# Attention and long-convolution kernel: block parameters and exponents in one load each, query scores copied to SBUF before their maximum is subtracted

## The chip, the cores and the metric

The kernel runs on one core of a Trainium2 chip. The core has five engines that run side by side, each with its own instruction queue in program order: TensorE (PE, matrix products into PSUM; PEld is its weight load), VectorE (DVE), ScalarE (ACT), GpSimd (POOL) and SyncE (SP), which here issues every DMA. They wait for one another through semaphores. The metric is the device time of one execution in microseconds (us).

## What is computed

Two independent layers over 2048 positions and 576 channels; their outputs stand side by side in the result.

```python
def _A_ref(u, log_A_real, A_imag, C_real, C_imag, log_dt, D_skip):
    dt = jnp.exp(log_dt)
    A = -jnp.exp(log_A_real) + 1j * A_imag
    C = (C_real + 1j * C_imag) * dt[:, None]
    P = jnp.exp((A * dt[:, None])[:, :, None] * pos[None, None, :])
    K = 2.0 * jnp.einsum("dn,dnl->dl", C, P).real          # 128 states n
    y = irfft(rfft(u_t, 4096) * rfft(K, 4096))[:, :, :2048]  # long convolution
    return y + u * D_skip

def _B_ref(x, wqkv, w_phi, wo):                 # 32 heads of 18
    q, k, v = split_heads(x @ wqkv)
    pq, pk = q @ w_phi, k @ w_phi               # per head
    phi_q = concat([softmax(pq), softmax(-pq)])
    phi_k = concat([softmax(pk), softmax(-pk)])
    kv, z = phi_k^T v, sum(phi_k)
    return (phi_q kv / (phi_q z + 1e-6)) @ wo
```

## The kernel before

**Attention layer.** The positions are cut into 16 tiles of 128. First `fold` multiplies `w_phi` into the key weights, and `whole` loads the value weights; each weight is split into a high part `wh` and a low part `wl` so that the fast float format keeps its precision. A key tile (`key_tile`) loads x (`zo`), splits it into the nine blocks `x9`, makes its scores and values in three matrix products of 14 passes each (378, 378 and 396 columns), takes both softmaxes (`softmax`) and adds its part to the state `kvt` with 32 small matmuls (`e,v` in the profile). After the sixteenth, the query weights are folded. A query tile (`query_tile`) makes its scores in two products of 288 columns, goes through `softmax(..., total=True)`, turns the result (L678), multiplies it with the state (`kvb,fT`), divides, turns it again (L706, L707) and multiplies with `wo`.

In `softmax`, DVE reads a half of the scores from PSUM three times: L568 takes the negated maximum, L569 the minimum, L570 (helper line L450) adds the negated maximum and writes the tile `e` in SBUF. L574 makes the mirrored half from it, L576 is the exponential on ACT.

**Convolution layer.** 144 matrices of 128 states are worked in 36 groups of four channels (`group`). A group's phases are made by integer additions on POOL (L888), turned into sines and cosines on ACT (L912 to L916), and weighted by magnitudes: three matmuls of the exponents `mg` with a selection matrix `sel` (L929), an exponential on ACT (L930) and four multiplications on DVE (L936 to L941). 64 small matmul passes (`E,cs`) make the group's part of the filter. Six blocks of six groups share parameters: `params` loads four rows of numbers per block (`dt`, `th`, `cre`, `cim`) with four DMAs and works on them with some forty small instructions; `exponents` loads `mg` twice, into the upper and the lower 64 partitions, from the array `gd` in device memory. The filter goes through a first transform step (`k_first`), u through `u_first`, then come 16 `product` blocks and 16 `last` blocks.

**What sets the order.** Nothing runs in the order in which it is written. A planner (`Plan.run`) holds all operations with their dependencies and costs and places them one after the other; each unit has a due time in the table `WANT`, each step of a unit an offset in `LEAD`, and `STAY`, `TURNOVER`, `NEAR`, `LEAN_POOL` and `LEAN_ACT` weigh the choices. An operation that names two engines (`copy("any", ...)`: ACT or DVE; `FLEX` and other pairs: DVE or POOL) is put where the planner sees it end first. Where the planner sees PE wait for the input of a new PSUM tile, it fills the wait with matmuls on zeros (L215, `ps<-ident,zero` in the profile), which compute nothing that is used. Each engine then runs its list in that fixed order.

Of the kernel before, what the change touches and what calls it, by code (L numbers as in the profile page):

```python
# [19 lines left out]
H, DH = 32, 18  # L20
# [28 lines left out]
def layouts(i):  # L49
# [4 lines left out]
    for g, n in enumerate(GRP):  # L54
# [3 lines left out]

    twice = lambda x: np.concatenate([x, x[512:]])
    lar, cre, cim = i["A_log_A_real"], i["A_C_real"], i["A_C_imag"]  # L60
    return dict(
        u=c(i["A_u"][0].reshape(64, 16, 2, D).transpose(2, 0, 1, 3).reshape(128, 16 * D)), mag=np.stack([by_row(x) for x in (lar, cre, cim)]), ldt2=by_row(i["A_log_dt"][:, None]), aim=by_group(i["A_A_imag"]), cre=by_group(i["A_C_real"]),
        cim=by_group(i["A_C_imag"]), ldt=by_group(i["A_log_dt"][:, None])[0], dsk=c(i["A_D_skip"]),
# [4 lines left out]
def constants():  # L68
# [56 lines left out]
    none = np.zeros_like(at)  # L125
    sel = np.concatenate([np.concatenate([at, none, dn], 1), np.concatenate([none, up, none], 1)])
# [25 lines left out]
class Mark(Buf):  # L152


    def __init__(self):
        self.tag, self.writers, self.readers = None, [], []


class Plan:
# [26 lines left out]
    def op(self, eng, cost, fn, r=(), w=(), with_=(), early=0.0, table=None, busy=1.0, lock=False, mode=(128, 128), add=None):  # L186
# [12 lines left out]
        bufs = list({id(b): b for b in (*r, *w, *with_) if not isinstance(b, Mark)}.values())  # L199
# [176 lines left out]
def c_dma(nbytes, run=4096):  # L376
    return nbytes / run * (0.35 + 0.0029 * run)
# [5 lines left out]
STAY, TURNOVER, NEAR, LEAN_POOL, LEAN_ACT = 201.0337, 32.8045, 106.7441, -80.6454, 62.4245  # L383
LEAD = dict(g1=-171.8003, g2=572.2435, g3=151.3761, g4=545.6015, k1=48.5812, k2=-375.6500, k3=-757.7275, k4=-640.2771, l1=-1201.2185, p1=-789.5548, p2=-44.7091, p3=-18.2983, p4=-535.3487, q1=82.0847, q2=-177.3983, q3=-254.3079, q4=-403.9251, q5=-398.9575, q6=-829.6788, u1=458.1288, xd=-783.9802)
# [4 lines left out]
    ident=[-108.8011],  # L389
    fold=[-9953.8356, -10398.4174, -453.1777, 165.8967],  # L390
    start=[1616.5931],
    key=[-6472.8031, -3126.8062, -1314.3574, -3125.3684, -656.72, -499.3546, -3140.1215, -1712.5806, -2108.3757,
          -1097.3828, -995.3063, -3475.5769, -5054.2771, -1149.402, -2645.614, -12059.5893],
    kv=[-10.1299],
    query=[5165.3029, 1080.554, 692.3202, 1735.0859, -197.7761, 3588.2092, 2132.912, 435.8626, 2776.5646, 4448.3212,
          4159.3881, 4303.4831, 5219.083, 4714.8471, 4446.1239, 3107.4294],
    u=[-1640.9461, -3267.9218, -4820.103, -2553.3502, -977.4058, -3531.8924, -390.5478, -577.8274, -2654.6962,
          -4160.3913, -2177.6267, -4468.1255, -741.7491, -4170.1538, -4622.046, -4241.0767],
    mags=[-9388.2816],
    sel=[-7210.3842, -4975.1123, -11383.6242],  # L400
    dsk=[2087.7151],
    par=[-11102.6929, -5509.5329, -1199.9769, -424.7275, 1524.2103, 2698.0598],
    group=[-7457.0019, -5406.6149, -4731.1573, -4251.2752, -3514.0599, -2749.8781, -3073.1041, -3256.4294, -3042.7242,
          -2141.1152, -1003.1983, -2662.6797, -315.8551, -156.0662, 211.9443, 4253.1033, 2854.2949, 574.2642],
    kfirst=[-4429.7629, -1297.4347, -385.4741, 1666.6694],
    product=[-90.1674, 1697.6391, -210.3218, 1304.2139, 977.2179, -172.77, 437.5617, -517.2988, 1754.78, 1904.223,
          3993.8576, 2617.1633, 3713.9029, 3193.0326, 3608.0088, 3162.4523],
    last=[2342.2332, 1752.2374, 2676.4796, 653.6455, 734.6483, 754.2121, 126.96, 2202.2106, 3127.1116, 3903.7028,
          3067.4349, 3943.3771, 2944.3536, 3914.8745, 4473.7986, 2888.4515],
)  # L410


def body(tc, nc, i, out, ctx):
    pl = Plan()
# [704 lines left out]
```

## Time and profile before

| | |
|---|---|
| three runs | 588.89, 586.17, 588.4 us, median 588.4 |
| profiled execution, own time | 588.28 us |
| its span, first to last instruction | 586.5 us |
| PE, DVE, ACT, POOL busy | 556.6, 513.1, 389.5, 251.8 us |
| zero matmuls of L215 | 193, busy 27.74 us of PE's 556.6 |
| mean granted TensorE clock | 0.991 |

"Busy" counts from the start of an instruction to its end, with overlaps counted once. Matmuls overlap, so the start-to-start distance says what one more costs. The page's slices are fortieths of the span (14.7 us); a digit 9 means 90% busy or more. The chain is the row of pieces of work, each released by the one before, that ended last. In the views of groups the columns are line, engine, operation, tiles, shapes and count; then busy time and mean length of one; then the idle time before them.

### The profile page before, as it was taken

Reading aid. Unit: us, or ns where it says so; the run is one execution under the profiler, and the core shown is the slowest. Engines: PE = TensorE matmul, PEld = TensorE weight load, DVE = VectorE, ACT = ScalarE, POOL = GpSimd, SP = SyncE. Lnnn points to the kernel's source line nnn. Section 1 sums busy time; section 2 is a strip of 40 time slices with the busy share of each in tenths; the row PEclk is TensorE's granted clock in tenths of the full one; section 3 lists DMA queues with packets and bytes.
Section 4 is the critical chain, followed back from the end, with each engine's and each line's share of the span. In section 5 each row is a group of like instructions: output and inputs, shape, how many; then the busy total and the mean of one; then the engine's idle time right before and its main releaser. Section 6 shows DMA issues by size and latency. Waiting matters only on the chain.

```text
span 586.5 us, 18741 instructions
## 1 busy us (share of the span) xinstructions
PE 556.6 (95%) x7657; PEld 457.9 (78%) x7657; DVE 513.1 (87%) x1109; ACT 389.5 (66%) x666; POOL 251.8 (43%) x393
## 2 busy tenths in 40 slices
PE   5998999999999899899999999999999999999996
PEld 3998989898879688778888766676788876767884
DVE  5789999999999899799999999799979797777751
ACT  5567767898579978578789777595955444432342
POOL 0448388682383656670566750674300201211000
PEclk9899999999999999899999999999999999999999
DMA  8977521457156767315867466975685799997587
GB/s 250 293 271 233 179 92 45 157 204 253 53 141 205 227 204 212 103 54 128 244 208 209 137 199 163 313 241 160 203 272 180 190 281 305 321 302 253 182 258 207
DMA packets 91316, 119.24 MB, mean 203 GB/s; under 512 B 9826, under 2 KB 73186, under 8 KB 91230
## 3 DMA queue, kind: packets, MB, share of 16 engines
q1 hardware_dynamic: 91230, 118.04, 65.1%
q8 instruction: 60, 0.98, 0.8%
q14 instruction: 26, 0.21, 0.1%
HBM read 68.76 MB, written 49.26 MB: 201 GB/s over the span
## 4 chain that ended last, share of the span: by engine, by line
PE 53%; DVE 24%; DMA 10%; ACT 5%; issue 3%; POOL 2%; SPq 2%; DVEq 0%; ACTq 0%; POOLq 0%
PE ps L431 49%; DVE E L937 3%; DVE e L446 3%; DMA zi<-dram 2%; DVE cs L936 2%; PE ps L678 2%; DMA out_dram<-yo 2%; DVE E L941 1%; DVE E L939 1%; DMA e<-in_wkT_dram 1%; DVE small L580 1%; DVE small L568 1%; PE ps L215 1%; DVE zi L436 1%; DVE e L450 1%
## 5 line engine op out<-in xcount | busy, mean ns | idle before, releaser
L431 PE MATMUL ps<-wh,x 128*128 128x288 f32 (+2 forms) x1008 | 241.8, 320 | 2.5 <-DVE zi L436 1.6
L431 PEld LDWEIGHTS ps<-wh,x 128*128 128x128 f32 x1008 | 174.2, 189 | 14.5 <-issue 6.7
L431 PE MATMUL ps<-wl,x 128*128 128x288 f32 (+2 forms) x560 | 175.5, 314 | 0.0
L888 POOL TENSOR_TENSOR cs<-cs,pi 128x32 int32<-128x32 int32 (+4 forms) x180 | 113.5, 639 | 9.4
L431 PEld LDWEIGHTS ps<-wl,x 128*128 128x128 f32 x560 | 106.4, 190 | 0.7
L579 POOL TENSOR_TENSOR o<-e 128x576 f32<-128x576 f32 x32 | 43.1, 1352 | 98.6 <-ACT e L576 77.1
L930 ACT ACTIVATE ps<-ps 128x512 f32<-128x512 f32 x108 | 56.6, 583 | 10.8 <-PE ps L431 9.7
L431 PEld LDWEIGHTS ps<-kvb,fT 126*128 126x128 f32 (+1 forms) x320 | 39.6, 192 | 8.8 <-issue 2.5
L450 DVE TENSOR_TENSOR ac<-us,ps 128x576 f32<-128x576 f32 x64 | 44.5, 743 | 1.4 <-ACT fT L436 1.1
L431 PE MATMUL ps<-E,cs 128*32 128x64 f32 x2304 | 42.4, 223 | 2.8 <-DVE E L941 1.8
L431 PE MATMUL ps<-kvb,fT 126*128 126x133 f32 (+1 forms) x320 | 42.8, 283 | 1.9 <-ACT fT L436 1.9
L431 PEld LDWEIGHTS ps<-E,cs 128*32 128x32 f32 x2304 | 35.6, 111 | 11.5 <-DVE E L941 4.1
L936 DVE TENSOR_TENSOR cs<-ps,cs 128x1024 f32<-128x1024 f32 x36 | 43.6, 1211 | 1.0 <-ACT ps L930 0.8
L937 DVE TENSOR_TENSOR E<-ps,cs 128x1024 f32<-128x1024 f32 x36 | 43.4, 1207 | 0.1
L446 POOL TENSOR_TENSOR ac<-ac 128x288 f32<-128x288 f32 x19 | 15.3, 805 | 65.2 <-DVE ac L450 65.1
L576 ACT ACTIVATE e<-e 128x1152 f32<-128x1152 f32 x32 | 37.4, 1179 | 5.4 <-POOL e L446 1.9
L436 ACT ACTIVATE ot<-ps 128x288 f32<-128x288 f32 x29 | 11.9, 416 | 40.8 <-PE ps L431 39.8
L912 ACT ACTIVATE cs<-cs 128x1040 f32<-128x1040 int32 x36 | 38.3, 1063 | 0.2
L431 PE MATMUL ps<-sel,mg 128*128 128x512 f32 x108 | 35.4, 428 | 2.8 <-ACT zi L436 1.7
L905 ACT ACTIVATE cs<-cs 128x1040 f32<-128x1040 int32 x31 | 33.1, 1070 | 5.7 <-POOL cs L888 5.7
L916 ACT ACTIVATE cs<-cs,hp 128x1040 f32<-128x1040 f32 x31 | 35.6, 1149 | 0.0
L431 PE MATMUL ps<-kb,fk 128*64 128x288 f32 x256 | 35.4, 414 | 0.1
(141 smaller groups left out, 1058.6 us busy)
## 6 DMA issues: line engine op xcount, KB each, us to landing
xd<-x SPq DMA_DIRECT2D x16, 576.0 KB
dram<-zi SPq DMA_DIRECT2D x16, 576.0 KB
dram<-zi SPq DMA_DIRECT2D x32, 288.0 KB
x<-xd SPq DMA_DIRECT2D x16, 576.0 KB
kb<-dram SPq DMA_DIRECT2D x32, 288.0 KB
ub<-dram SPq DMA_DIRECT2D x32, 288.0 KB
dram<-zo SPq DMA_DIRECT2D x32, 288.0 KB
zi<-dram SPq DMA_DIRECT2D x16, 576.0 KB
```

The lines of the kernel that those rows point to most:

```text
L431: pe.matmul(o, l, r, start=start, stop=stop, skip_group_check=skip)
L446: op(eng, [c_dve(n[0]) if e == "dve" else c_pool(n[1]) for e in eng], lambda e: (dve if e == "dve" else pool).tensor_tensor(dst(), a(), b( ...
L450: op(eng, c_dve(n) if eng == "dve" else c_pool(n), lambda: e.tensor_tensor(dst(), a(), b(), op=alu), r=r, w=w, lock=eng == "pool" or not a ...
L576: op("act", c_act(1152) + 40, lambda: act.activation(e.t, e.t, AF.Exp), r=[e], w=[e], table="exp")
L579: op("pool", c_pool(470), lambda: pool.tensor_tensor(pair.t, e.t[:, :, :, 0:9], e.t[:, :, :, 9:18], op=ALU.add), r=[e], w=[pair], lock=True)
L888: op("pool", c_pool(2 * n * W), lambda n=n, j=j: pool.tensor_tensor(x()[:, :, :, n:2 * n], x()[:, :, :, 0:n], pi.t[:, j:j + 2, gs].bitcast ...
L905: act.activation(cs.t[:, 0], x(), AF.Abs)
L912: act.activation(cs.t[:, 1], cs.t[:, 1].bitcast(I32), AF.Sin, scale=TURN)
L916: act.activation(cs.t[:, 0], cs.t[:, 0], AF.Sin, scale=-TURN, bias=hp.t)
L930: op("act", c_act(512), lambda: act.activation(ps.t, ps.t, AF.Exp), r=[ps], w=[ps], table="exp")
L936: op("dve", c_dve(64 * W), lambda: dve.tensor_tensor(F(), both(M.t), F(), op=ALU.mult), r=[M, cs], w=[cs])
L937: op("dve", c_dve(64 * W), lambda: dve.tensor_tensor(E.t[:, :, :, 32:64], both(up.t), cs.t[:, :, :, 0:32], op=ALU.mult), r=[up, cs], w=[E])
```

## The change

Four edits. (1) A block's four parameter rows come in one DMA of 1536 bytes per partition into a tile `four` of four parts; the host lays them out as one array, with `log_dt` repeated for all partitions. (2) `mg` is loaded once, as 72 rows: 64 as before and 8 rows of zeros that a new DMA writes into `gd` once at the start; `sel` shrinks to 72 rows accordingly and its columns stand plainly side by side. (3) In the softmax of the query tiles, ACT copies each half of the scores from PSUM into `e`, and the negated maximum is added there, SBUF to SBUF, by DVE or POOL as the planner sees fit. Maximum and minimum are still read from PSUM by DVE. The key tiles are as before. (4) The whole table of due times and weights has other numbers, so every engine's list has another order.

```diff
-        ... ldt2=by_row(i["A_log_dt"][:, None]), aim=by_group(i["A_A_imag"]), cre=by_group(i["A_C_real"]),
-        cim=by_group(i["A_C_imag"]), ldt=by_group(i["A_log_dt"][:, None])[0], dsk=c(i["D_skip"]),
+        ... ldt2=by_row(i["A_log_dt"][:, None]), four=four,
...
-    sel = np.concatenate([np.concatenate([at, none, dn], 1), np.concatenate([none, up, none], 1)])
+    sel = np.concatenate([np.concatenate([at, up, dn], 1), np.zeros((8, 1536))])
...
-STAY, TURNOVER, NEAR, LEAN_POOL, LEAN_ACT = 201.0337, 32.8045, 106.7441, -80.6454, 62.4245
+STAY, TURNOVER, NEAR, LEAN_POOL, LEAN_ACT = 114.4459, 2.6100, 30.1761, -108.2709, 139.8883
...
-    start=[1616.5931],
+    start=[-7842.1222],
...
-            tt("dve", lambda: e.t[:, 0, hs, :], v, lambda: ends.t[:, :, 0:1].to_broadcast([128, m, DH]), ALU.add, [p, ends], [e], DH * m)
+            if total:
+                copy("act", lambda: e.t[:, 0, hs, :], v, [p], [e], DH * m)
+                tt(FLEX, lambda: e.t[:, 0, hs, :], lambda: e.t[:, 0, hs, :], lambda: ends.t[:, :, 0:1].to_broadcast([128, m, DH]), ALU.add, [e, ends], [e], (DH * m, DH * m - 60))
+            else:
+                tt("dve", lambda: e.t[:, 0, hs, :], v, lambda: ends.t[:, :, 0:1].to_broadcast([128, m, DH]), ALU.add, [p, ends], [e], DH * m)
...
-    gd = B("gd", [4 * W, 40, NS])
+    gd = B("gd", [4 * W + 8, 40, NS])
+    op("sp", 640 * 1.1, lambda: sp.dma_start(gd.t[64:72].rearrange("r g n -> (r g n)").rearrange("(p k n) -> p k n", p=128, k=5),
+                                              pl.zero.t.bitcast(F32)[:, None, :].to_broadcast([128, 5, 64])), r=[pl.zero], w=[gd])
...
-        mg = B("mg", [128, NG // NB, NS], F32R)
-        for h in range(2):
-            op("sp", c_dma(64 * 3072), lambda h=h: sp.dma_start(
-                mg.t[64 * h:64 * h + 64].bitcast(F32), gd.t[:, NG // NB * blk:NG // NB * (blk + 1)]), r=[gd], w=[mg])
+        mg = B("mg", [4 * W + 8, NG // NB, NS], F32R)
+        op("sp", c_dma(72 * 3072), lambda: sp.dma_start(mg.t.bitcast(F32), gd.t[:, NG // NB * blk:NG // NB * (blk + 1)]), r=[gd], w=[mg])
...
-        op("sp", 300, lambda: sp.dma_start(dt.t, i["ldt"][cs].rearrange("(o d) -> o d", o=1).to_broadcast([128, BW])), w=[dt], early=8)
-        for b, n in ((th, "aim"), (cre, "cre"), (cim, "cim")):
-            op("sp", 300, lambda b=b, n=n: sp.dma_start(b.t, i[n][:, cs]), w=[b], early=8)
+        four = B("dt", [128, 4, BW])
+        dt, th, cre, cim = (Part(four, k) for k in range(4))
+        op("sp", c_dma(128 * 1536, 1536), lambda: sp.dma_start(
+            four.t.rearrange("p k n -> p (k n)"), i["four"][:, 4 * BW * blk:4 * BW * (blk + 1)]), w=[dt, th, cre, cim], early=8)
```

What the new numbers do to the lists is seen at three places. The first is SP's list at the very start, before the change: x of the first key tile (`zo`) is the first load, the four parameter rows follow, then the value weights (`zi`, `cs`), the folding weights (`fT`, `e`).

```order
L473 DMA zo<-in_xT_dram 128x5x128
L802 DMA v_97<-in_sel_dram 128x512
L821 DMA dt<-in_ldt_dram 128x96
L823 DMA th<-in_aim_dram 128x96
L823 DMA cre<-in_cre_dram 128x96
L823 DMA cim<-in_cim_dram 128x96
L473 DMA zi<-in_wv_dram 128x5x192 x2
L473 DMA cs<-in_wv_dram 128x5x192
L482 DMA fT<-in_wphi_dram 128x630
L486 DMA e<-in_wkT_dram 126x640 x2
```

After the change, the same list from the last key weights (`kvb`) on, its twelfth DMA:

```order
L500 DMA kvb<-in_wkT_dram 72x640
L785 DMA ld<-in_ldt_dram 128x5
L790 DMA gd<-zero 640x1x64
L798 DMA ac<-in_mag_dram 128x640 x2
L798 DMA ks<-in_mag_dram 128x640
L822 DMA v_159<-in_sel_dram 72x512
L487 DMA zo<-in_xT_dram 128x5x128
L764 DMA ub<-in_u_dram 128x576
L747 DMA w_211<-in_w_dram 128x192
```

The first tile of x has moved from the first load to the nineteenth, behind all key weights, the zeros for `gd` and the magnitudes.

The second place is DVE's list in a query tile late in the groups, before the change: maximum and minimum (L568, L569), the subtraction that reads PSUM (L450), the sum of both ends (L571), the mirrored half (L446).

```order
L568 TENSOR_REDUCE small<-ps 128x16
L569 TENSOR_REDUCE small<-ps 128x16
L450 TENSOR_TENSOR e<-ps,small 128x288
L571 TENSOR_REDUCE small<-small 128x16
L446 TENSOR_TENSOR e<-small,e 128x576
```

After the change, at a like place:

```order
L582 TENSOR_REDUCE small<-ps 128x16
L583 TENSOR_REDUCE small<-ps 128x16
L460 TENSOR_TENSOR e<-e,small 128x288
L450 COPY zi<-ps 128x8x36
L589 TENSOR_REDUCE small<-small 128x16
L460 TENSOR_TENSOR e<-small,e 128x576
```

The subtraction has kept its place on DVE and reads `e` and `small` in SBUF; 27 of the 32 stay there, 5 go to POOL. ACT's list has 32 new copies, here one (`e<-ps`) in front of other PSUM copies:

```order
L450 ACTIVATE ot<-ps 128x288
L453 ACTIVATE e<-ps 128x288
L450 ACTIVATE ks<-ps 128x64x4
L450 ACTIVATE zo<-ps 128x288 x2
L948 ACT_TABLE_LOAD
```

The third place is the end of PE's list. Before, with the last query tiles (`e`, `fT`, `o` are steps of one query tile, `zi,w` the last transform):

```order
L678 MATMUL ps<-ident,e 126x128 x8
L431 MATMUL ps<-zi,w_258 64x288 x8
L678 MATMUL ps<-ident,e 72x128 x2
L706 MATMUL ps<-ident,o 128x128 x4
L707 MATMUL ps<-ident,o 128x128
L431 MATMUL ps<-kvb,fT 128x133 x8
L431 MATMUL ps<-kvb,fT 128x76 x2
```

After, at the same step of the last query tile:

```order
L696 MATMUL ps<-ident,e 126x128 x4
L445 MATMUL ps<-zi,w_216 64x288 x4
L696 MATMUL ps<-ident,e 126x128 x4
L696 MATMUL ps<-ident,e 72x128 x2
L229 LDWEIGHTS zero
L229 MATMUL ps<-ident,zero 64x256
L445 MATMUL ps<-zi,w_216 64x288 x4
L445 MATMUL ps<-kvb,fT 128x133 x8
L445 MATMUL ps<-kvb,fT 128x76 x2
```

There are zero matmuls at the very end where there were none: 12 behind the last group, and 253 in all against 193. Of these, 78 against 66 stand ahead of the steady run of key products, 100 against 47 from there to the 18th group, and 63 against 80 from the 18th to the 36th. In the whole lists, DVE has 1095 instructions against 1111, ACT 721 against 668 (40 table loads against 34), SP 374 against 397.

70 lines of the change are left out of this document (39 added, 31 removed).

## The prediction

> **What bounds the kernel.** I read the page first, for which engine has no room:
>
> ```profile
> span 586.5 us, 18741 instructions
> PE 556.6 (95%) x7657; PEld 457.9 (78%) x7657; DVE 513.1 (87%) x1109; ACT 389.5 (66%) x666; POOL 251.8 (43%) x393
> PE   5998999999999899899999999999999999999996
> DVE  5789999999999899799999999799979797777751
> PE 53%; DVE 24%; DMA 10%; ACT 5%; issue 3%; POOL 2%; SPq 2%; DVEq 0%; ACTq 0%; POOLq 0%
> ```
>
> PE is full from the second slice to the last, but 27.7 us of that are zero matmuls, which stand where the planner saw PE wait. DVE is full beside it for three quarters of the span, and the chain that ended last (last row) passes through PE and DVE. So I cut the span where the kind of limit changes: the start (to 28.8 us, where the key products run without a break), to the 18th group's end (258.3), to the 36th group's (454.2), and the finish. The first four rows are all engines (span, then PE, PEld, DVE, ACT and POOL busy), the next four the zero matmuls alone:
>
> ```profile
> 0.00:28.80 28.80, 21.55 (x134) 19.44 (x135) 17.72 (x49) 15.59 (x29) 6.89 (x21) 0.88 0.93 272
> 28.80:258.30 229.50, 219.47 (x3335) 194.74 (x3332) 218.53 (x458) 175.98 (x271) 142.44 (x216) 0.99 0.53 167
> 258.30:454.20 195.90, 189.25 (x2847) 146.19 (x2840) 185.70 (x390) 150.09 (x258) 86.26 (x143) 1.00 0.66 200
> 454.20:581.30 127.10, 126.35 (x1353) 97.52 (x1353) 90.70 (x214) 47.80 (x110) 16.21 (x15) 1.00 0.84 261
> ...
> 0.00:28.80 28.80, 9.70 (x66) 7.54 (x66) 0.88 0.93 272
> 28.80:258.30 229.50, 7.08 (x50) 4.32 (x47) 0.99 0.53 167
> 258.30:454.20 195.90, 10.95 (x80) 7.52 (x80) 1.00 0.66 200
> 454.20:581.30 127.10, 0.00 (x0) 0.00 (x0) 1.00 0.84 261
> ```
>
> The start is DMA's (share 0.93). In the second stretch PE has 17.1 us without real work (10.0 idle, 7.1 of zeros), DVE has 11.0 idle of 229.5: DVE is the tighter one. In the third PE has 17.6 (6.65 idle, 10.95 zeros), DVE 10.2: both are tight. In the finish PE has 0.75 of 127.1 and no zeros: PE alone, and its work there cannot be shortened by any other engine.
>
> **The change, part by part.** The groups by shape give the prices:
>
> ```profile
> L450 DVE TENSOR_TENSOR e<-ps,small 128x288 f32<-128x288 f32 x32 | 14.1, 442 | 0.1
> L446 DVE TENSOR_TENSOR ac<-ac 128x288 f32<-128x288 f32 x45 | 20.7, 484 | 0.1
> L446 DVE TENSOR_TENSOR e<-e,small 128x1152 f32<-128x1152 f32 x13 | 18.6, 1437 | 0.0
> L446 DVE TENSOR_TENSOR x<-zo,x 128x512 fp32r<-128x512 f32 x9 | 8.0, 891 | 4.4 <-ACT x L525 4.3
> L446 DVE TENSOR_TENSOR x<-zo,x 64x128 fp32r<-64x128 f32 x7 | 3.3, 472 | 0.2
> L834 DVE TENSOR_SCALAR dt<-ax 128x96 f32<-128x96 f32 x18 | 5.6, 309 | 0.0
> L436 DVE COPY zi<-ps 128x288 f32<-128x288 f32 x62 | 25.2, 444 | 4.9 <-PE ps L431 4.7
> L446 POOL TENSOR_TENSOR ac<-ac 128x288 f32<-128x288 f32 x19 | 15.3, 805 | 65.2 <-DVE ac L450 65.1
> L436 ACT ACTIVATE zi<-ps 128x288 f32<-128x288 f32 x66 | 23.2, 421 | 13.1 <-PE ps L431 11.3 <-ACT fT L436 0.9 <-ACT cs L905 0.4
> L912 ACT ACT_TABLE_LOAD x14 | 18.0, 1283 | 0.2
> ```
>
> The scores: 32 subtractions at 0.442 us leave DVE and 27 at 0.484 (the nearest SBUF-to-SBUF operation of that size, `ac`) come back: 14.1 against 13.1, a gain of 1.0 us. POOL gets 5 at 0.805, 4.0 us on an engine with 335 us free. ACT gets 32 copies at 0.421, 13.5 us. So the edit itself hardly relieves DVE; what counts is how the new table shares out the rest. Counting both lists stretch by stretch, at these prices:
>
> To the 18th group, DVE's additions: the low parts of x (two more of 0.891, three of 0.472) +3.2; value copies of three key tiles moved from ACT, about two of 0.444 each, +2.7; three `ks` copies of 256 columns +1.2; two 576-wide products at half of 1.437, +1.4; most of a fifth block's parameters, done before instead of behind this point, +4.5 (some 15 small ones at the 0.309 of `dt`). Off: two 1152-wide products −2.9, two `zi` copies −0.9, query subtractions −0.2. Sum +9.0. Means overlap (over all DVE groups of this view, means times counts add to 585 us against 513.1 busy), so times 0.88: +7.9. The 4.0 of it that are parameters may lie in the 11.0 us that DVE idles; the rest has no cover, since PE needs it (DVE's results feed the key state and the groups). I take +3.9, ends 0 and +7.9. PE's list has 53 more zero matmuls there, which agrees in sign; they stand in those waits and are not added again.
>
> From the 18th to the 36th group DVE has −1.8 (10 subtractions of 0.484 for 15 of 0.442), −4.4 (ten `zi` copies), −2.7 (six other copies to ACT), −1.0 (two `ac`), −4.5 (the parameters) and −2.1 in small ones: −16.5, times 0.88 is −14.5 us. But PE takes over as the limit. Behind the 18th group it has 56 more products of 288 columns to do, and less of other things. Its prices, from the finish, where nothing stands between them:
>
> ```profile
> 560.13 2.41 PE L431 MATMUL ps<-kvb,fT 126*128 126x133 f32 x20
> 562.38 1.04 PE L678 MATMUL ps<-ident,e 128*126 128x128 f32 x8
> 573.33 0.40 PE L431 MATMUL ps<-wh,x 128*128 128x288 f32 x1
> 579.11 2.16 PE L431 MATMUL ps<-zi,w 128*64 128x288 f32 x16
> ```
>
> From 573.33 to 579.11 stand 42 products, 0.138 each: 56 are 7.7 us. Off go 10 transposes (0.13 each, 1.3), 12 `kvb` passes (0.12, 1.4) and one u tile (about 1.2): +3.8. By the 36th group it is ahead of before by 20 `kvb` passes and five transposes, 3.0. Real work: 189.25 − 10.95 + 3.8 + 3.0 = 185.1; 63 zeros at 10.95/80 = 0.137 add 8.6: 193.7; of the idle 6.65 I leave half, since DVE is late less often: 197.0, or +1.1 against 195.9. Ends: all idle kept, +4.5; zeros and idle both gone, 185.1, −10.8.
>
> The finish: 3.0 us of it are done earlier, 12 zeros stand in it, 1.6: −1.4; ends −3.0 and +1.6. They stand before steps of the last query tile, whose chain has nothing else beside it.
>
> The start: before, 2208 KiB (`zo`, `sel`, four parameter rows, three value weights) were landed at 11.82, when ACT could split the last value weight, and 960 KiB of these from 8.49 on, 3.33 us.
>
> ```profile
> 8.49 1.00 ACT L513 ACTIVATE wh<-zi 128x960 fp32r<-128x960 f32 x1 [1.96 <-DMA zi<-in_wv_dram]
> 11.82 1.00 ACT L513 ACTIVATE wh<-cs 128x960 fp32r<-128x960 f32 x1 [0.83 <-DMA cs<-in_wv_dram]
> 14.36 2.05 PE L431 MATMUL ps<-fT,e 126*128 126x126 f32 x8 [5.65 <-DMA e<-in_wkT_dram]
> 26.70 2.36 PE L215 MATMUL ps<-ident,zero 128*128 128x256 bf16 x20
> 28.79 0.19 PEld L431 LDWEIGHTS ps<-wh,x 128*128 128x128 f32 x1
> ```
>
> Now 5405 KiB lie up to and with the first x: 3197 more at 288 KiB/us, landed at 22.9. Splitting it (ACT and DVE, about 2 us) and one u tile put the first key product at 25.7. Before, the steady run began at 28.8 with 28 products done (4.9 us at full clock) and one fold block (1.1) still to do, as if at 25.0; now it begins at 25.7 with a u tile (1.2) done, as if at 24.5. I take 0; ends −1 and +2 (the rate may fall with the 640 short rows of zeros).
>
> ACT gets, beside the 13.5, some fifteen copies that DVE gave up (6) and six table loads (7.7): 27 us, on an engine 66% busy. Most lies beside PE; the chain holds ACT for 5%, so +1.4; ends 0 and +7.7, the table loads in full. A query copy can also stand at the head of ACT's queue waiting for its scores, with `ks` and `zo` copies behind it that PE waits for; that is inside these ends.
>
> The loads: 18 fewer DMAs for parameters, 6 fewer for `mg`. SP is never named on the chain for more than 2%. What they cost is seen where a parameter came late:
>
> ```profile
> ACT dt L827 <- DMA dt<-in_ldt_dram: 2.4, 2, 1.5
> ACT ax L827 <- DMA cre<-in_cre_dram: 1.0, 1, 1.0
> ACT ay L827 <- DMA cim<-in_cim_dram: 0.5, 1, 0.5
> 65.28 4.33 DMA cim<-in_cim_dram
> ```
>
> ACT idled 3.9 us for them in all; the chain has one with 4.33. What would be late next is the magnitudes and PE, so I count −1.0; ends −3.9 and 0. [...]
>
> **Sum.** +3.9 + 1.1 − 1.4 + 0 + 1.4 − 1.0 = +4.0. The profiled execution took 588.28, which is 1.8 above its span and 0.1 below the median of 588.4: 592.3 us.
>
> **Rivals.** *DVE's relief is felt in full.* If the third stretch is DVE's rather than PE's, it shrinks until real PE work is all that is left, −10.8 instead of +1.1: 588.28 + 3.9 − 10.8 − 1.4 + 1.4 − 1.0 = 580.4. It decides when PE's zeros there lie inside waits for DVE that would vanish. For it: DVE busy 185.7 of 195.9 and only 6.65 us of PE idle. Against it: the zeros stay in the list and run whether needed or not.
>
> *Everything hides.* PE's real work is the same in both, and the added zeros and DVE work lie in idle time: 588. Against it: DVE has only 11.0 us idle in the second stretch.
>
> *DVE and POOL get in each other's way.* The rows that compare:
>
> ```profile
> L446 DVE TENSOR_TENSOR ac<-ac x45: 381/448/1344, 322.7 to 543.2; 128x288 f32<-128x288 f32 x45
> L446 DVE TENSOR_TENSOR e<-small,e x27: 686/757/1850, 43.5 to 556.2; 128x576 f32<-128x576 f32 x27
> L450 DVE TENSOR_TENSOR e<-ps,small x64: 298/446/553, 28.4 to 555.6; 128x288 f32<-128x288 f32 x32, 128x378 f32<-128x378 f32 x16, 128x198 f32<-128x198 f32 x16
> ```
>
> Lengths are minimum, median, maximum in ns. Operations with both inputs in SBUF sometimes take three times their median (1344 against 448), those with one input in PSUM never (553, and that at 378 columns). The 27 moved subtractions join the first kind. If each is held up for half of the 0.9 us that the worst was, DVE has 12 us more; with half of that on the path and the queue of ACT behind it, 592.3 + 6 = 598.3. Against it: the median is unmoved and the mean, 484, is already in the sum. [...]
>
> *The first x comes late.* It stands behind 5405 KiB; if the rate falls by a tenth it comes 1.1 us later, and the fold and split work of ACT and DVE piles up before it: +2 to +3, 595.
>
> **Chances.** Forecast 592.3 with its own range 588 to 596: 0.40. Relief felt, 580.4: 0.26. Hidden, 588: 0.15. Contention, 598.3: 0.12. Late start, 595: 0.07. About 0.5% (2.9 us) is what this measurement can tell from no change, so the line to "slower" is 591.3 and to "faster" 585.5. Faster: the relief, 0.26. Same: the hidden case and a quarter of the forecast, 0.25. Slower: the rest, 0.49. The range 580 to 602 leaves out the lower part of the relief case and the upper part of contention. All upper ends together (+4.0, +3.4, +3.0, +2.0, +6.3 and +1.0 more than the terms taken) would give 612; that they all meet is unlikely.
>
> **What would show it.** DVE's busy time near 507 us and ACT's near 414; the zero matmuls near 34 us; the 18th group ending near 262 and the 36th near 460; the first steady key product near 25.7; in the finish, PE idle or on zeros by about 2 us where it had 0.75. Wrong: the 36th group ending before 450 would mean that DVE, not PE, held the third stretch; the 18th ending before 258 that the added DVE work was covered; a mean of the moved subtraction above 0.55 us that contention is real.

## The result and the profile after

The changed kernel takes 603.79 us (median of four runs, 601.77 to 604.92) against 588.18 for the kernel before: a ratio of 1.026, 95% interval 1.0226 to 1.0294. The direction was forecast; the 15.6 us are four times the +4.0 of the sum, and outside the range. The profiled execution took 604.61 us, its span 602.8. One of the four executions of E3 and two of the ten of E14 below were slow ones, which the ratios leave out.

Line numbers of the changed kernel: L582 and L583 are maximum and minimum of the scores, L453 ScalarE's copy, L460 element-wise operations in SBUF (the moved subtraction among them), L464 those with PSUM, L445 matmuls, L229 the zeros. The page first:

```profile
span 602.8 us, 18864 instructions
...
PE 566.9 (94%) x7717; PEld 466.1 (77%) x7717; DVE 513.1 (85%) x1093; ACT 412.2 (68%) x719; POOL 253.8 (42%) x394
...
PE 60%; DVE 19%; DMA 9%; ACT 7%; issue 3%; SPq 1%; POOL 0%; ACTq 0%; DVEq 0%
```

DVE's busy time is what it was, its share of the chain fell from 24% to 19%, PE's rose to 60%. Then the same cut as before: to the steady run of PE (25.4), the 18th group, the 36th, the last product; all engines, then the zero matmuls alone.

```profile
0.00:25.40 25.40, 18.72 (x129) 16.71 (x131) 17.06 (x47) 14.59 (x26) 5.45 (x19) 0.87 0.93 282
25.40:264.10 238.70, 227.50 (x3379) 201.30 (x3376) 228.60 (x487) 184.38 (x287) 138.68 (x212) 0.99 0.50 161
264.10:465.60 201.50, 193.66 (x2881) 152.05 (x2873) 174.23 (x346) 161.58 (x286) 95.87 (x152) 0.99 0.63 188
465.60:597.80 132.20, 127.00 (x1344) 96.03 (x1340) 92.77 (x215) 51.70 (x122) 13.77 (x13) 1.00 0.81 257
...
0.00:25.40 25.40, 10.17 (x78) 8.10 (x78) 0.87 0.93 282
25.40:264.10 238.70, 12.46 (x102) 9.47 (x100) 0.99 0.50 161
264.10:465.60 201.50, 8.23 (x63) 5.77 (x63) 0.99 0.63 188
465.60:597.80 132.20, 2.05 (x12) 1.00 (x12) 1.00 0.81 257
```

The 16.3 us of span come in three nearly equal parts: +5.8 by the 18th group (258.3 to 264.1), +5.6 from there to the 36th (195.9 to 201.5), +5.1 in the finish (127.1 to 132.2); the tail behind PE's last product is 0.2 shorter. By kind they are +5.2 of zeros (27.73 to 32.90), +6.0 in which PE is idle (span less PE busy, 29.9 to 35.9), and +5.1 of PE time for the same real products. Most of the last is the clock of this execution, which these rows show, behind the start, in the one place where it halves before (first fence) and in one of three after (second):

```profile
240.00:242.00 2.00, 0.77 (x5) 0.78 (x6) 0.36 (x1) 1.44 (x3) 1.24 (x1) 0.94 0.82 287
242.00:244.00 2.00, 2.00 (x25) 1.86 (x27) 1.35 (x5) 0.00 (x0) 2.00 (x2) 0.50 0.00 0
244.00:246.00 2.00, 2.00 (x63) 1.82 (x55) 1.01 (x4) 1.13 (x2) 0.44 (x4) 0.71 0.00 0
```

```profile
372.00:374.00 2.00, 1.56 (x10) 1.59 (x11) 1.12 (x4) 1.98 (x4) 0.00 (x0) 0.84 0.00 1
374.00:376.00 2.00, 2.00 (x22) 1.38 (x21) 0.57 (x2) 1.57 (x4) 0.00 (x0) 0.50 0.87 186
376.00:378.00 2.00, 2.00 (x26) 1.48 (x11) 2.00 (x2) 1.32 (x4) 0.00 (x0) 0.81 0.41 107
```

The third number from the end is the clock. Missing clock times length is 2 x (0.16 + 0.50 + 0.19) = 1.7 us for a stretch of 3.4 us at half clock. The other two are at 62 to 67 and 140 to 145; two more than before make 3.4 us. That share changes from one execution to the next: the four of the changed kernel have mean clocks of 0.984, 0.985, 0.991 and 0.992 and took 604.92, 604.61, 602.96 and 601.77 us. What stands ahead of the one at 374, on PE, DVE and ACT (start, length, instruction, idle before it):

```profile
369.78 0.86 PE L445 MATMUL ps<-ks,w 32*64 32x288 f32 x16
372.44 0.37 PE L445 MATMUL ps<-wh,x 128*128 128x288 f32 x1 [1.81 <-DVE small L583]
```

```profile
370.90 0.46 DVE L582 TENSOR_REDUCE small<-ps 128x16 f32<-128x288 f32 x1
371.84 0.46 DVE L583 TENSOR_REDUCE small<-ps 128x16 f32<-128x288 f32 x1 [0.48 <-ACT e L453]
```

```profile
371.39 0.41 ACT L453 ACTIVATE e<-ps 128x288 f32<-128x288 f32 x1 [1.56 <-DVE small L582]
```

PE needs a PSUM tile that still holds query scores. DVE's maximum reads it at 370.90; the copy waits until the maximum is done, the minimum until the copy is done, though all three only read. The tile is free half a microsecond late, which is 0.48 of PE's 1.81 us; the rest is the late maximum. This wait is not in the prediction. Over the whole kernel (who waited for whom: total, times, longest):

```profile
ACT e L453 <- DVE small L582: 22.7, 10, 6.6
...
DVE small L583 <- ACT e L453: 4.9, 10, 0.5
...
DVE small L582 <- ACT e L453: 1.3, 3, 0.5
```

In E1 below, where the copies read SBUF, none of these three rows is left: it is the copies' reading of the scores' PSUM tile that brings the waits. Why two reads of one tile wait for each other is shown by no run.

### The profile page after: what moved, and what is told of

The parts are those of the page before. It is cut to its first block, busy times and chain, and to the rows that moved or that the text cites. A ratio compares the mean times of both kernels' runs of the same rounds, so it can differ in the third digit from the quotient of the medians.

```text
span 602.8 us, 18864 instructions
## 1 busy us (share of the span) xinstructions
PE 566.9 (94%) x7717; PEld 466.1 (77%) x7717; DVE 513.1 (85%) x1093; ACT 412.2 (68%) x719; POOL 253.8 (42%) x394
## 4 chain that ended last, share of the span: by engine, by line
PE 60%; DVE 19%; DMA 9%; ACT 7%; issue 3%; SPq 1%; POOL 0%; ACTq 0%; DVEq 0%
PE ps L445 56%; DMA zi<-dram 3%; DVE e L460 3%; PE ps L229 2%; DVE E L955 2%; DMA e<-in_wqT_dram 2%; PE ps L696 2%; ACT ps L948 2%; DVE ac L464 1%; DVE cs L954 1%; DVE small L582 1%; DMA e<-in_wkT_dram 1%; DVE small L583 1%; DVE small L598 1%; DMA ub<-dram 1%
## 5 line engine op out<-in xcount | busy, mean ns | idle before, releaser
L445 PE MATMUL ps<-wh,x 128*128 128x288 f32 (+2 forms) x1008 | 245.1, 324 | 6.1 <-ACT us L450 2.3
L445 PEld LDWEIGHTS ps<-wh,x 128*128 128x128 f32 x1008 | 175.7, 191 | 21.9 <-issue 8.0
L445 PE MATMUL ps<-wl,x 128*128 128x288 f32 (+2 forms) x560 | 176.7, 316 | 0.0
L906 POOL TENSOR_TENSOR cs<-cs,pi 128x128 int32<-128x128 int32 (+4 forms) x180 | 117.5, 656 | 10.0
L445 PEld LDWEIGHTS ps<-wl,x 128*128 128x128 f32 x560 | 107.4, 192 | 0.6
L464 DVE TENSOR_TENSOR ac<-us,ps 128x576 f32<-128x576 f32 x64 | 44.3, 743 | 3.4 <-PE ps L445 2.7
L445 PE MATMUL ps<-E,cs 128*32 128x64 f32 x2304 | 41.4, 221 | 3.4 <-DVE E L957 2.3
L445 PEld LDWEIGHTS ps<-E,cs 128*32 128x32 f32 x2304 | 34.8, 110 | 12.4 <-DVE E L959 3.6
L460 DVE TENSOR_TENSOR e<-e,small 128x288 f32<-128x288 f32 (+2 forms) x53 | 42.5, 805 | 1.0 <-ACT e L453 0.6
L445 PEld LDWEIGHTS ps<-kvb,fT 126*128 126x128 f32 (+1 forms) x320 | 39.0, 188 | 4.6 <-issue 2.2
L445 PE MATMUL ps<-kvb,fT 126*128 126x133 f32 (+1 forms) x320 | 41.3, 278 | 0.0
L460 POOL TENSOR_TENSOR ac<-ac 128x288 f32<-128x288 f32 x21 | 16.8, 808 | 54.0 <-DVE ac L464 37.0
L582 DVE TENSOR_REDUCE small<-ps 128x21 f32<-128x378 f32 (+1 forms) x64 | 28.7, 449 | 11.9 <-PE ps L445 9.5
L445 PE MATMUL ps<-sel,mg 72*128 72x512 f32 x108 | 35.8, 429 | 2.5 <-DVE zi L450 1.1
```

The costliest lines, as they stand in the source:

```text
L445: pe.matmul(o, l, r, start=start, stop=stop, skip_group_check=skip)
L460: op(eng, [c_dve(n[0]) if e == "dve" else c_pool(n[1]) for e in eng], lambda e: (dve if e == "dve" else pool).tensor_tensor(dst(), a(), b( ...
L464: op(eng, c_dve(n) if eng == "dve" else c_pool(n), lambda: e.tensor_tensor(dst(), a(), b(), op=alu), r=r, w=w, lock=eng == "pool" or not a ...
L582: op("dve", c_dve(DH * m), lambda: dve.tensor_reduce(ends.t[:, :, 0], v(), axis=AX.X, op=ALU.max, negate=True), r=[p], w=[ends])
L906: op("pool", c_pool(2 * n * W), lambda n=n, j=j: pool.tensor_tensor(x()[:, :, :, n:2 * n], x()[:, :, :, 0:n], pi.t[:, j:j + 2, gs].bitcast ...
```

## Experiments

Theories: **A**, the copies of the scores cost, by the order on the PSUM tile (A1) or otherwise (A2); **B**, the new order of the lists costs; **C**, PE's waits set the clock to half; **D**, the added zeros stand in PE's way; **E**, numbers and code fit only as a pair. Most kernels keep all lists as they are and change only what one instruction does, since any change to an operation's cost or tiles makes the planner lay out all lists anew. Ratios are to the kernel before, on the same chip, with 95% intervals.

### E1, E2: the changed order, without the PSUM order and without the copies

E1, in `part` of `softmax`:

```diff
-                copy("act", lambda: e.t[:, 0, hs, :], v, [p], [e], DH * m)
+                copy("act", lambda: e.t[:, 0, hs, :], lambda: wqo[0].t[:, 0, 0:DH * m].bitcast(F32)..., [p], [e], DH * m)
```

> The changed kernel with every engine's list as it is, but ScalarE's 32 score copies read an SBUF tile instead of the PSUM scores, so that they cannot be ordered behind DVE's maximum and minimum on the same PSUM tile (the query scores are left out of the result). Theory A, the wait between ScalarE and DVE on one PSUM tile: in the changed kernel it idled ScalarE 22.7 us and DVE 6.2 us, and one PSUM slot released by a late minimum stopped PE for 1.81 us at 372.44; without it at least a third of the 15.6 us comes back, 598.5 us or less, and no PE wait names the minimum L583. Theory B, the new order of the lists is what costs: these waits lie beside other work, 602 to 605 us. Theory C, the half-clock stretches of PE cost: the one at 372.44 goes (1.7 us), the two before it stay, about 602.

E2 (`keep` is true in the five places that GpSimd subtracts):

```diff
-                copy("act", lambda: e.t[:, 0, hs, :], v, [p], [e], DH * m)
-                tt(FLEX, lambda: e.t[:, 0, hs, :], lambda: e.t[:, 0, hs, :], ...
+                op("act", c_act(DH * m), lambda: act.activation(e.t[:, 0, hs, :], v(), AF.Copy) if keep else None, r=[p], w=[e])
+                tt(FLEX, lambda: e.t[:, 0, hs, :], lambda: e.t[:, 0, hs, :] if keep else v(), ...
```

> The changed kernel with every engine's list as it is, but the third edit is taken back in 27 of 32 places: ScalarE's copy is not issued and DVE subtracts straight from PSUM at the place where it subtracted in SBUF (the five that GpSimd does keep the copy). The result is whole. Theory A (the copies and their wait cost): 598.5 us or less; ScalarE busy falls by 27 x 0.41 = 11 us to about 401. Theory B (the order costs, the edit itself nothing): 602 to 605 us. Against both: PSUM tiles are now held until the late subtraction, 2 to 44 places further down the lists, which may cost PE slots: then above 605, and PE's waits name L589 or the subtraction.

E1 took 599.07 us, 1.0197 (1.0144 to 1.025); E2 596.61, 1.0156 (1.0098 to 1.0214). E2's interval lies just clear of the changed kernel's 1.0226 to 1.0294: in this order the copies (27 of the 32) cost about 1.04%, 6 to 7 us of the 15.6. E1 lies between; its interval overlaps both, so that the PSUM order is more than half of it (4.7 of 7.2 by the medians) is likely, not settled. In the profiled executions DVE begins the 36th group's products at 460.59 in the changed kernel, 455.99 in E1 and 456.08 in E2: up to there E1 is as far ahead as E2, and the two part in the finish. The half-clock stretch at 374 is gone in both; PE still waits once for a minimum in E1 (1.24 us, and the clock stays up), in E2 never. E2 by stretches, all engines, then zeros:

```profile
25.40:261.90 236.50, 225.86 (x3379) 199.55 (x3375) 228.44 (x487) 182.84 (x282) 138.34 (x212) 0.99 0.51 164
261.90:461.20 199.30, 193.81 (x2877) 151.34 (x2873) 174.19 (x347) 157.76 (x275) 95.33 (x152) 1.00 0.63 192
461.20:590.00 128.80, 126.50 (x1340) 95.83 (x1340) 91.88 (x214) 47.72 (x111) 13.91 (x13) 1.00 0.82 260
...
sum 590.00, PE 33.98 PEld 24.90; mean PE 8.50 PEld 6.23
```

Against the changed kernel's rows, 2.2 us come off ahead of the 18th group, 2.2 in the third stretch and 3.4 in the finish, where PE's idle time falls from 5.2 to 2.3. The first 2.2 are not all the copies' price. The first copy in the changed kernel starts at 231.48, and by then E2 is already 1.5 us ahead, on instructions that are the same in both: the 15th group's products begin on DVE at 228.44 and 226.93, and most of this stands at one wait of PE for query weights (2.10 us at 223.46 against 1.16). Such a difference is one of executions, not of the edit. Some 8.5 us over the kernel before stay, of which 6.2 are zeros (33.98 against 27.73).

### E3, E4: without the zeros

```diff
-            for _ in range(fill):
+            for _ in range(0):
```

> The changed kernel without the zero matmuls (32.9 us busy), lists else as they are. Theory D, the 5.2 us of zeros more than before simply stand in PE's way: at least 5 us faster, 598 us or less. Theory B: they stand where PE waits anyway, and time stays within 3 us of 603.8. Theory C, the zeros keep the clock up: without them more stretches of some 3.4 us at a clock of 0.50, each costing 1.7 us; the mean clock falls below 0.985 and the time rises by 3 us or more.

> The kernel before without its zero matmuls (27.7 us busy), lists else as they are. Theory D: faster by about as much per us of zeros as in the changed kernel, 583 to 585 us. Theory B: within 3 us of 588.2. Theory C: slower, with a clock below 0.991 and more stretches at 0.50; if it loses more than the changed kernel does, the zeros before stood in better places.

The changed kernel without its 253 zeros took 604.75 to 610.92 us, 1.0332 (1.0257 to 1.0408); the kernel before without its 193 took 590.43, 1.005 (1.0014 to 1.0085). Theory D falls: taking 33 us of zeros away makes nothing faster. Their greater number says that PE has more to wait for in the new lists, not that they cost. For theory C, the clock of the changed kernel does fall (0.969 to 0.982 over the executions, 0.984 to 0.992 with the zeros). In the kernel before it does not clearly fall: 0.988 against 0.991 in the two profiled executions, but 0.989 against 0.990 as means over all executions.

### E5, E9, E14: the third edit alone, in the old order

E5 adds ScalarE's copy to the kernel before and lets DVE subtract in SBUF. The lists are kept by planning first and issuing afterwards; `flag` is set in the 29 places where a tile `e` is free early enough.

```diff
+                dve.tensor_reduce(ends.t[:, :, 0], v(), axis=AX.X, op=ALU.max, negate=True)
+                if flag:
+                    act.activation(e.t[:, 0, hs, :], v(), AF.Copy)
...
+                if total and not flag:
+                    act.activation(e.t[:, 0, hs, :], v(), AF.Copy)
+                dve.tensor_tensor(e.t[:, 0, hs, :], e.t[:, 0, hs, :] if total else v(), ends...to_broadcast([128, m, DH]), op=ALU.add)
```

> The kernel before with the third edit alone and every other instruction where it was: ScalarE copies each half of the query scores (in 29 of 32 places issued right behind the maximum, in three behind the minimum), and DVE subtracts in SBUF at the place where it subtracted from PSUM. PE's, GpSimd's and the DMA lists are the same as before. Theory A (the copies and their wait cost in any order): in the changed kernel the third edit was worth 603.8 - 596.6 = 7.2 us, so 593 to 597 us here. Theory B' (they cost only in the new order, which puts them badly): within 2 us of 588.

E9 is E5 with the copies reading `wqo` as in E1 (the query scores are left out); E14 has only the copies, from `wqo` to a tile of their own, and the old subtraction.

> As the kernel before with the third edit alone (609.55 us), all lists the same, but the copies read an SBUF tile instead of the PSUM scores, so that the minimum need not follow them (the query scores are left out of the result); the subtraction still waits for the copy. Theory A1, the order on the PSUM tile costs (there DVE's minimum waited 19.1 us for copies, 3.6 at the longest at 273.60, and PE stood 2.17 us for that minimum and then ran at half clock to 282): most of the 20.7 us goes, 589 to 594 us, no PE wait on the minimum, a clock back near 0.99. Theory A2, the copies' 32 x 0.41 us on ScalarE and DVE's wait in front of the subtraction cost: 600 us or more stay.

> The kernel before with 32 copies more on ScalarE, at the places where the third edit alone had them, from an SBUF tile into an SBUF tile that nothing reads or waits for; DVE subtracts from PSUM as before, the result is whole. With the copies read from SBUF and DVE's subtraction behind them the loss was 12.3 us (598.94 against 586.64). Theory A2a, ScalarE's added 13 us is the loss: 596 to 600 us. Theory A2b, DVE's wait for the copy is the loss: 587 to 590 us.

E5 took 609.55 us, 1.0348 (1.0305 to 1.0392); E9 598.94, 1.0194 (1.0153 to 1.0235); E14 585.81 to 594.09, 1.0047 (1.0008 to 1.0086). The intervals are apart, so the third edit's 3.48% in the old order (20 us, more than the whole change) divide into three: ScalarE's added time 0.47% (2.8 us, with an interval of 0.5 to 5), DVE's dependence on the copy together with its dearer subtraction 1.47% (some 8.6 us), the order on the PSUM tile 1.54% (some 9 us). E5's worst place, on DVE, ACT and PE:

```profile
269.59 0.45 DVE L597 TENSOR_REDUCE small<-ps 128x16 f32<-128x288 f32 x1
273.60 0.46 DVE L603 TENSOR_REDUCE small<-ps 128x16 f32<-128x288 f32 x1 [3.56 <-ACT e L599]
```

```profile
272.13 1.14 ACT L954 ACTIVATE cs<-cs,hp 128x1040 f32<-128x1040 f32 x1
273.18 0.38 ACT L599 ACTIVATE e<-ps 128x288 f32<-128x288 f32 x1
```

```profile
270.91 1.04 PE L716 MATMUL ps<-ident,e 128*126 128x128 f32 x8
274.11 0.41 PE L716 MATMUL ps<-ident,e 128*72 128x128 f32 x2 [2.17 <-DVE small L603]
```

The copy stands in ScalarE's queue behind sines and cosines of a microsecond each. So DVE stands 3.56 us for its minimum, PE 2.17 us for the PSUM tile, and then the clock halves for 6.8 us; from the windows of E5:

```profile
274.00:276.00 2.00, 0.89 (x4) 0.44 (x4) 2.00 (x8) 0.04 (x1) 0.00 (x0) 0.80 0.00 0
276.00:278.00 2.00, 1.73 (x8) 1.49 (x8) 1.99 (x9) 0.80 (x2) 0.00 (x0) 0.50 0.00 0
278.00:280.00 2.00, 2.00 (x11) 2.00 (x10) 1.45 (x3) 0.07 (x1) 0.00 (x0) 0.50 0.13 25
280.00:282.00 2.00, 2.00 (x11) 2.00 (x10) 1.10 (x4) 1.10 (x2) 0.00 (x0) 0.50 0.00 0
```

E5 has four such places (224, 276, 320, 372), together 10.2 us of missing clock; E9 has 3.4 us of it ahead of the finish. So between these two profiled executions, whose spans are 11.0 us apart, 6.8 us are missing clock; over all executions the mean clocks, 0.981 and 0.986, differ by less than in these two (0.976 and 0.988). The middle part is visible in E9's waits (first fence), in its groups (second) and beside these in E14's groups (third):

```profile
DVE e L606 <- ACT e L598: 7.6, 3, 3.0
```

```profile
L606 DVE TENSOR_TENSOR e<-e,small 128x288 f32<-128x288 f32 x32 | 19.0, 595 | 8.3 <-ACT e L598 7.6 <-ACT e L605 0.6
```

```profile
L459 DVE TENSOR_TENSOR e<-ps,small 128x288 f32<-128x288 f32 x32 | 14.2, 444 | 0.1
```

DVE waits 8.3 us for the copies, and the subtraction itself takes 595 ns instead of 444. The longer mean goes with GpSimd's work beside it: in E9, the 19 subtractions beside which GpSimd is busy for less than a tenth of their time have a mean of 443 ns, and the 11 beside which it is busy for more than half have 872; in E14, with one input in PSUM, the same two means are 443 (17) and 445 (15).

### E10, E15, E16: other places for the copy

E10 is E5 with the copy behind the minimum. E15 (changed kernel) and E16 (E5) put it ahead of the maximum and read all three from SBUF:

```diff
+                if flag:
+                    act.activation(e.t[:, 0, hs, :], v(), AF.Copy)
+                dve.tensor_reduce(ends.t[:, :, 0], e.t[:, 0, hs, :] if flag else v(), axis=AX.X, op=ALU.max, negate=True)
```

> As the kernel before with the third edit alone, but each copy is issued behind the minimum instead of between maximum and minimum (29 of 32 as before, three unchanged); PE's, DVE's, GpSimd's and the DMA lists stay. A1: the minimum is no longer held up, but the subtraction is, and the PSUM tile is free only after the copy, so part of the loss stays: 596 to 606 us, with DVE's waits for ScalarE moved from the minimum to the subtraction. If the place of the copy does not matter, 609 again.

> The changed kernel, lists of PE, GpSimd and DMAs the same, but each copy is issued ahead of the maximum (31 of 32 places) and DVE takes maximum, minimum and difference from the copy in SBUF; no two engines share the scores' PSUM tile. If the order on the PSUM tile is the harm (4.7 of the 7.2 us): 597 to 600 us. If DVE's wait for the copy is as bad wherever it stands: 604 or more, since the wait now stands ahead of three instructions.

> The kernel before with the third edit alone and the copy ahead of the maximum (29 of 32), maximum, minimum and difference from SBUF; other lists as before. With the copy behind the maximum it was 609.55. If the order on the PSUM tile is the harm: 597 to 600, as when the copies read SBUF; if DVE's wait for ScalarE's queue is: 605 to 612.

E10 took 607.32 us, 1.0341 (1.0302 to 1.0381): no better than E5; DVE's wait moved from the minimum to the subtraction (18.8 us). E16 took 601.44, 1.0233 (1.0192 to 1.0274): better than E5, near E9, and between the two ranges that were expected. E15 took 610.33, 1.0377 (1.0325 to 1.0429): worse than the changed kernel, as expected if DVE's wait is as bad wherever it stands. With no shared PSUM tile DVE waits for the copy itself, E15 first, then E16:

```profile
DVE small L615 <- ACT e L614: 27.5, 18, 4.4
```

```profile
DVE small L598 <- ACT e L597: 18.4, 13, 4.0
```

None of the places that were tried made the copy free. Ahead of the maximum, ScalarE itself often stands idle for the scores (23.0 us, 14 times in E15), and DVE begins only when the copy behind them is done.

### E6, E7: numbers and code

E6 is the kernel before with the new table, E7 the changed code with the old one.

> The kernel before, all four old edits' code, with the numbers of the new table (the planner then lays out other lists than in either kernel). Theory B, the new numbers make worse lists: 594 us or more, near the 596.6 that was left in the new order without the copies. Theory E, the lists are only as good as the fit between numbers and code: also slower, and then the next run is slower than 603.8 - 7.2 as well.

> The changed code with the old numbers. Theory B, the new numbers are what costs beside the copies: 588 + 7 = 595 us or less. Theory E, any numbers that were fitted to other code give worse lists: above 597, as slow as the changed kernel or slower.

627.82 us, 1.0685 (1.0625 to 1.0745), and 642.92, 1.092 (1.0877 to 1.0964). Theory E: each table suits only its own code, so these runs price neither the table nor the code, and theory B can be neither shown nor refuted by them.

### E8, E13: the loads

E8 issues four parameter loads and two of `mg` at the places of one each in the changed kernel; E13 has the first two edits alone in the old order, with three of a block's four parameter rows in one load and the fourth in its own.

```diff
+            sp.dma_start(dt.t, i["ldt"][cs].rearrange("(o d) -> o d", o=1).to_broadcast([128, BW]))
+            for b, n in ((th, "aim"), (cre, "cre"), (cim, "cim")):
+                sp.dma_start(b.t, i[n][:, cs])
```

> The changed kernel with the first two edits taken back as far as DMA issues go: four parameter DMAs and two of the exponents per block, at the places of the one load each, 24 DMAs more; all other lists the same. I predicted that the fewer loads give 1.0 us (0 to 3.9), so 604.8 (603.8 to 607.7). Against it: in the changed kernel ScalarE still waits 3.8 us for parameters, against 3.9 before, so nothing was gained, 603.8 within 1.5 us.

> The kernel before with the first two edits alone, every engine's list as before but for the loads: three of a block's four parameter rows come in one DMA (the fourth keeps its own, since the lists' tiles don't allow one for all), the exponents once as 72 rows, the zeros written once, sel of 72 rows: 18 DMAs fewer and one more. My term was -1.0 (0 to -3.9): 587 us, or 585 to 588. Against it: in the changed kernel ScalarE still waited 3.8 us for parameters; then 588 within 1 us.

E13 took 588.67 us, 1.0008 (0.9979 to 1.0038): no gain is seen there, and the interval (−1.2 to +2.2 us) allows one of 1.2 us at most. E8 took 607.07, 1.0311 (1.027 to 1.0353); that is 3.3 us more than the changed kernel by medians, with overlapping intervals, so a gain of up to that size in the new order isn't excluded.

### E11, E12: zeros against the half clock

```diff
-            self.emit(k, o, e, nf)
+            self.emit(k, o, e, nf + {1483: 9, 134: 9, 1599: 9}.get(k, 0))
```

(E12, in the kernel before: `{714: 17}`.)

> The changed kernel with 27 zero matmuls more, nine each ahead of the selection matmul before the wait at 61.9, of the key product before the wait at 133.5 and of the selection matmul before the wait at 139.4, about 1 us of PE time each. Theory C, a PE wait of some 2 us in a short time sets the clock to 0.50 for 3.4 us, 1.7 us lost each time, and zeros ahead of the wait prevent it: the stretches near 64 and 142 are gone, the clock is 0.99, and the time falls by 1 to 3.4 us. Without theory C the zeros are 3 us more work ahead of DVE's: 604 to 607 us.

> The kernel before with 17 zero matmuls more (1.85 us) in the one wait before its one stretch at half clock, 1.95 us for ScalarE ahead of the state products at 241.23. Theory C: the wait is filled, the stretch at 242 to 245 goes and with it 1.7 us: about 586.5 us. Otherwise 588 within 1 us.

E11 took 603.54 us, 1.0301 (1.0243 to 1.0358): no gain. The stretches near 64, 142 and 374 are gone and the 18th group ends at 262.4 instead of 264.1; but PE's idle time in the finish is longer and another half-clock stretch stands at 490. E12 took 589.75, 1.0035 (1.001 to 1.006), and says nothing of theory C, because the zeros ended up behind the wait instead of in it:

```profile
241.03 0.73 PE L431 MATMUL ps<-kvb,fT 126*128 126x133 f32 x4 [1.95 <-ACT fT L436]
241.59 3.13 PE L215 MATMUL ps<-ident,zero 128*128 128x256 bf16 x17
```

The wait stayed, and 17 zeros took 3.13 us, 0.18 us each, in windows with a clock of 0.58 and 0.57 (242 to 246); 13 zeros from 231.47 on, at a clock of 1.00, took 1.59 us, 0.12 each.

No kernel here beats the one before; E13 equals it.

## Why the prediction was wrong

**The third edit was sized at a fifth of its price.** The sum gave it a gain of 1.0 us on DVE, within the counts of the stretches, and +1.4 on ScalarE (six table loads and some fifteen other copies included), and put a query copy that waits at the head of ACT's queue inside the ends of that term (0 to +7.7). Measured, E2: 6 to 7 us in the new order, near that upper end. The step that failed is the term for ScalarE: it asked how long the copies take and what waits in ScalarE's queue, and not who on DVE waits for the copies. Minimum (through the PSUM tile, 4.9 us in the changed kernel) and subtraction (through `e`, 0.6 us) both do. ScalarE's own time was right, 412.2 us busy against 414 forecast, and by itself it costs 0.47% (E14).

**To the 18th group**, +3.9 forecast, +5.8 measured. The start came as forecast (PE runs steadily from 25.4, the first key product in that run starts at 26.48; forecast 25.7). With the cut at 28.8 in both, DVE's work to the 18th group grew by 7.45 us (218.53 to 225.98) against 7.9 forecast. DVE had 11.0 us idle there before, and 4.0 us of parameters were to lie in it; 9.3 are left, so 1.7 did. Without the copies (E2) the 18th group ends at 261.9, +3.6, near the term. Of the 2.2 us between E2 and the changed kernel, 1.5 are there before the first copy and belong to the one profiled execution; at most 0.7 are the copies'.

**The third stretch**, +1.1 forecast, +5.6 measured, beyond its upper end of +4.5. PE's real work was forecast at 185.1 and is 193.66 − 8.23 = 185.4; the zeros at 8.6, and are 8.23. The step that failed is "of the idle 6.65 I leave half, since DVE is late less often": PE is idle 7.84 where 3.3 were left, which is the whole error of the stretch. DVE did get 11.5 us less to do (14.5 forecast), but PE waits there for PSUM tiles and results at single places, and the copy made one of these later (1.81 us at 372.44, 1.24 in E1, none in E2). Without the copies (E2) PE's idle time is 5.5, so halving it fails there too. The agreement in real work is partly luck, since 1.7 us of it are the stretch at half clock.

**The finish**, −1.4 forecast, +5.1 measured, beyond its upper end of +1.6. The zeros came as counted (12, 2.05 us), real work is less by 1.4 instead of 3.0 (126.35 to 124.95), and PE is idle 5.2 us where it had 0.75. That no idle time would appear was taken for granted because there was none. The waits that appear are for loads:

```profile
PE ps L445 <- DMA zi<-dram: 3.5, 3, 1.6
...
PE ps L445 <- DMA ff<-in_ff_dram: 1.3, 1, 1.3
```

E2 takes 3 us of this idle time away with the loads unchanged, so the late query tiles are behind most of it. How the rest comes about isn't shown.

**The loads**, −1.0 forecast: E13's −1.2 to +2.2 us neither shows this nor rules it out. What did not come is that fewer loads shorten ScalarE's wait for parameters in the changed kernel. It was 3.9 us and is

```profile
ACT dt L845 <- DMA dt<-in_four_dram: 3.8, 2, 2.6
```

**The rivals.** The relief of DVE (580.4) fell, but not for the reason in the text against it, that the zeros run whether needed or not: without them (E3) nothing is faster. "Everything hides" (588) falls with the measured time, and the late first x with the start, which came as forecast. Contention of DVE and GpSimd was to show as a mean of the moved subtraction above 0.55 us; in the changed kernel it is

```profile
L460 DVE TENSOR_TENSOR e<-e,small 128x288 f32<-128x288 f32 x27 | 13.5, 504 | 0.7 <-ACT e L453 0.6
```

but in the old order 595 (E9). The two means of E9 (443 and 872 ns) show longer subtractions beside a busy GpSimd; in the changed kernel GpSimd is busy for more than half of the time of only six of the 27. Why DVE's total did not fall to 507 as forecast is not worked out; single shapes went both ways (18 operations of 96 columns from 267 to 422 ns, 12 others from 322 to 251).

**What stays open:** some 8.5 us of the new order that are neither copies nor loads (E2 against before). They show as 6.2 us more of zeros, that is as waits that the planner foresaw, and E6 and E7 say that the numbers can't be judged apart from the code. What the new order costs, and by which waits, is therefore not shown.

## What to carry to other kernels

When an engine is added as a reader of a PSUM tile, price the waits on both sides of it, reader against reader, and not the added instruction: here 32 copies of 0.41 us cost, in the old order, 2.8 us by their own time and some 17.6 more by who stood behind them and by the dearer subtraction. An engine with microsecond-long instructions in its queue is a bad place for a short step on which a busier engine depends: in E5 the copy came behind one of 1.14 us, and DVE stood 3.56. In a kernel whose order comes from a fitted table, a change is best tried with the order held, one instruction's work at a time; a new order and an edit can't be told apart by exchanging tables.

## What the runs showed of the hardware beyond that

In the start, the clock of TensorE fell while PE waited, 5.65 us before (0.77 from 12 to 14, 0.50 from 14 to 18) and 5.08 in the changed kernel (0.88 from 10 to 12, 0.50 from 12 to 18). Later it fell to 0.50 for stretches of 3.4 us, or twice that (6.8 us in E5), after waits of about 2 us: 1.95 us in one piece before, 1.81 in the changed kernel (ahead of the one at 374), 1.00 and 1.07 six microseconds apart (ahead of the one at 142), 0.68 and 1.09 two and a half apart (ahead of the one at 64). Each stretch of 3.4 us takes 1.7 us of PE's clock, as worked out above for the one before. A wait of about 2 us doesn't always do it: 2.10 us at 223.46 in the changed kernel left the clock at 1.00, and so did 0.99 and 1.07 us at the same two places in E2. The kernel before waits 1.74 us at 195 and keeps 1.00, while in E12, after 1.73 us at the same place, the clock falls to 0.51. The length of the wait alone doesn't decide, and these runs don't show what else does.

Two operations in SBUF at the same moment, one on DVE and one on GpSimd, both took longer than the others of their shape. In the changed kernel two of 1152 columns met once:

```profile
128.94 3.35 DVE L460 TENSOR_TENSOR e<-e,small 128x1152 f32<-128x1152 f32 x1
```

```profile
128.36 2.71 POOL L460 TENSOR_TENSOR e<-e,small 128x1152 f32<-128x1152 f32 x1
```

DVE's mean for this shape was 1437 ns before, and its ten others in the changed kernel took 1.35 to 1.56 us; GpSimd's four others took 2.19 to 2.20. Behind the 3.35 us comes one DVE product for whose PSUM tile PE then waits 1.00 us, the first of the two waits ahead of the stretch at 142.
